# Loads of v from the third pair on issued by GpSimd instead of SyncE, in a fused attention and mixture-of-experts kernel

## The chip, the cores and the metric

The kernel runs on one core of one Trainium2 chip. The metric is the device time of one execution in microseconds (us), the median of three runs. Times inside the kernel come from one profiled execution, counted from its first instruction.

## What is computed

Four batches of 12 heads of sigmoid attention over 448 tokens, then a soft mixture of eight experts, then a dense layer with g(h) = h cos h. All inputs and outputs are float32.

```python
scores = scale * np.matmul(q, k.transpose(0, 1, 3, 2)) - np.log(S)
attn = 1.0 / (1.0 + np.exp(-scores))
x = np.matmul(attn, v)                      # (4, 12, 448, 64) -> (1792, 768)
logits = x @ phi                            # 32 slots, softmax over tokens (d) and over slots (c)
slot_out = relu((d.T @ x) @ w1) @ w2        # per expert, 4 slots each
h = (c @ slot_out) @ w_in
out = (h * np.cos(h)) @ w_out
```

## The kernel before

**Work and stages.** Two heads make a pair, and the attention stage goes through 24 pairs (`attention`, line 691). For pair i, `scores` (L395) multiplies keys and queries in four groups of keys g = 0 to 3, ScalarE applies the sigmoid (`squash`, L403), and `attn_v` (L414) multiplies with v into a single PSUM tile `av`, which VectorE copies out (`keep_tokens`, L424, the tile xt) and transposes (L431). In between, at the end of each batch of six pairs, the statistics of the slot softmax are made (L445 to L676). After the attention stage come the experts (L957 to L1088: w1, then w2, at lines 972 and 1008) and the dense layer (L1161 on).

**What is loaded, and by whom.** SyncE (SP) issues every load, and one queue takes them in that order. For each pair there are two halves of keys and queries (`load_qk`, L353, tiles raw8_1 and so on, 224 KB each, three buffers and an early one) and one tile of v (`load_v`, L357, 224 KB). VectorE splits each raw half into two float16 parts (`cast_upper` L373, tile hi, and `cast_lower` L376, tile lo). Beside that, halves of w_in (tiles wi, 512 KB, L245) and of w1 (tiles w, 512 KB, L221) are fetched ahead; each piece of wi is narrowed from float64 by one ScalarE and three VectorE operations (L264 to L271).

**The tiles of v.** Pair i's v lies in the one buffer of the pool `v_even` or `v_odd` (L313, L317, L356), so that the load for pair i + 2 has to wait until pair i's last group of `attn_v` (g = 3, with the tile `one`) has read it. From then until `attn_v` of pair i + 2 begins is the time that a load has. ScalarE also copies two corners of a loaded v (`swap_tails`, L362), which group 3 uses.

**What sets the order.** A planner (`Plan`, L73) runs through the operations with costs and ranks and emits each engine's order before the chip sees any of it. In it the load of v for pair i + 2 follows `attn_v` of group 3:

```python
824:             if i + 2 < NP:
825:                 v[i + 2] = add("sp", .62, lambda i=i: load_v(i + 2), [chain], kind="v", kb=229)
```

On the chip SP waits at each issue until the buffer is free, and what stands behind it in SP's order waits too. A later load also waits until the load eight places earlier in the same issuer's order has landed.

Of the kernel before, what the change touches and what calls it, by code (L numbers as in the profile page):

```python
# [32 lines left out]
VW = 7 * D  # L33
# [125 lines left out]
def fused(ctx: ExitStack, tc: tile.TileContext, qk, vv, phi, w1, w2, w_in, w_out, out):  # L159
    nc = tc.nc  # L160
# [148 lines left out]
    with ExitStack() as at:  # L309
# [20 lines left out]
        raw, v32, hi, lo, aa = {}, {}, {}, {}, {}  # L330
# [23 lines left out]

        def load_v(i):
            v32[i] = vps[i % 2].tile([P, VW + D], F32, tag="v", name=f"v{i}")  # L356
            nc.sync.dma_start(out=v32[i][:, 0:VW], in_=vv[i])  # L357

        def swap_tails(i, k, copy=nc.scalar.copy):

# [330 lines left out]
        def attention():  # L691
# [86 lines left out]
            for _ in range(3):  # L778
                j, m = queue.pop(0)
                qk[j, m] = add("sp", .62, lambda j=j, m=m: load_qk(j, m), [room.pop(0), qk.get("last")], kind="qk", kb=229)  # L780
                qk["last"] = qk[j, m]
            v[1] = add("sp", .62, lambda: load_v(1), kind="v", kb=229)
            fill(0)
            def score(i, g):
# [26 lines left out]
            def value(i, g):  # L811
                nonlocal chain
                swaps = None
                b, hp = divmod(i, HP)
                if g == 3:
                    for k in range(2):
                        swaps = add("act", .17, lambda k=k: swap_tails(i, k), [v.get(i), swaps if k else None], kind="swap")
                chain = av[i, g] = add(
                    "pe", (.835, .74, .74, .37)[g], lambda i=i, g=g: attn_v(i, g),
                    [chain, sq[i, g], v.get(i) if g < 3 else swaps] + ([kept.get(i - 1)] if g == 0 else []),  # L820
                )
                if g < 3:
                    return
                if i + 2 < NP:
                    v[i + 2] = add("sp", .62, lambda i=i: load_v(i + 2), [chain], kind="v", kb=229)
                kept[i] = add(
                    "dve", .54, lambda i=i: keep_tokens(i),
                    [chain, turned.get(i - 3), read.get(i - 3), ready if i == NP - 1 else None], kind="tokens",
                )
                if i < NP - 1:  # L830
                    turned[i] = add(
                        "dve", .56, lambda i=i: turn_tokens(i),
                        [kept[i], turned.get(i - 1)] + [slot.get((k, b - 1)) for k in range(2) if hp == 0],
                        kind="turn",
                    )
                if hp == 2:
                    read_tokens(b, 0)
                if hp == HP - 1 and b < B - 1 or i == NP - 2:
                    batch(b)
# [36 lines left out]
        with tc.manual_schedule():  # L876
            nc.vector.memset(zeros, 0.0)
            warm_up(8, zeros)
            for k in (1, 0):
                load_qk(0, k)  # L880
            load_v(0)
            for k in (1, 0):
                load_qk(1, k)
            nc.sync.dma_start(out=phi_sb, in_=phi)
            nc.gpsimd.memset(bias_s, neg_log_s)
            warm = const.tile([P, 1], F32, name="warm")
            nc.scalar.activation(warm, bias_s, AF.Sigmoid)
            make_identity(nc, ident)
            two = midp.tile([P, S], F32, tag="ex", name="two")[:, 0:2 * NS]
            nc.vector.tensor_add(two, ident[:, 0:2 * NS], ident[:, 2 * NS:P])  # L890
            both = [two[:, k * NS:(k + 1) * NS].unsqueeze(1).to_broadcast([P, 4, NS]) for k in range(2)]
            nc.vector.tensor_add(fold4, *both)
            first_casts()
            attention()
# [552 lines left out]
```

## Time and profile before

| | us |
|---|---|
| median of 3 runs (lowest, highest) | 506.79 (506.06, 507.98) |
| the profiled execution | 508.52 |
| its span, first to last instruction | 506.7 |
| attention stage | about 5 to 153 |
| end of attention's statistics, first weights of the experts | 153 to 164 |
| experts | 164 to 240 |
| dense layer | 240 to 507 |

The profiled execution took 1.8 us more than its span, for what lies around the first and last instruction. A row of the page or of the trace names an engine, a line of the kernel, an operation and tiles as out<-in. An idle time in brackets stands before the instruction that ended it, with what released it. PE is TensorE, PEld its weight loads, DVE VectorE, ACT ScalarE, POOL GpSimd, SP SyncE; "SPq" is SP's issue of a DMA. The three engines PE, DVE and ACT were busy for 481.8, 325.5 and 292.3 us of the span, POOL for 0.7 us.

### The profile page before, as it was taken

What the parts mean: (1) busy time and instruction counts of PE and PEld (TensorE: products, weight loads), DVE (VectorE), ACT (ScalarE), POOL (GpSimd) and SP (SyncE); (2) the same over time, 40 slices, a digit from 0 to 9 for tenths busy, and PEclk for the clock granted to TensorE, in tenths of its full rate; (3) what the DMA queues carried; (4) which work ended last, traced back from release to release, by engine and by line L of the source; (5) the groups of instructions that cost most, each with busy time, mean ns of one, the idle gap of its engine ahead of it and who ended that gap; (6) DMA issues with size and microseconds to landing.
All of it is one profiled execution on the core that took longest, in us unless ns stands there. A gap on an engine that the chain in (4) does not pass through costs nothing.

```text
span 506.7 us, 11038 instructions
## 1 busy us (share of the span) xinstructions
PE 481.8 (95%) x4560; PEld 349.3 (69%) x4560; DVE 325.5 (64%) x655; ACT 292.3 (58%) x508; POOL 0.7 (0%) x7
## 2 busy tenths in 40 slices
PE   8998989999999998677999999999999999999997
PEld 5665556565565323222567999999999899899996
DVE  4898879999975063000689899996644654654442
ACT  5887858877861002000679889865655545555552
POOL 0000000000000000000000000000000000000000
PEclk9999999999999998999999999999999999999999
DMA  7999979979839999999824633000210110020003
GB/s 254 393 314 329 295 254 358 328 225 361 278 116 378 403 417 415 413 415 389 354 56 149 232 124 125 1 2 0 76 35 1 45 64 1 26 85 0 1 0 110
DMA packets 33442, 99.12 MB, mean 196 GB/s; under 512 B 3568, under 2 KB 17520, under 8 KB 33392
## 3 DMA queue, kind: packets, MB, share of 16 engines
q1 hardware_dynamic: 33392, 98.42, 53.3%
q8 instruction: 36, 0.59, 0.5%
q14 instruction: 14, 0.11, 0.1%
HBM read 92.11 MB, written 5.51 MB: 193 GB/s over the span
## 4 chain that ended last, share of the span: by engine, by line
PE 66%; DMA 18%; DVE 11%; ACT 2%; issue 2%; SPq 0%; DVEq 0%; ACTq 0%
PE o L1234 45%; DMA w<-in_w 14%; PE av L414 6%; PE sc L395 4%; DMA raw<-in_qk 3%; PE h L1199 3%; DVE lo L376 2%; PE sl L633 2%; DVE wi L268 1%; DVE hi L373 1%; PE idle L474 1%; DVE xt L424 1%; DMA wi<-in_w_in 1%; PE o L1219 1%; PE m L945 1%
## 5 line engine op out<-in xcount | busy, mean ns | idle before, releaser
L1234 PE MATMUL o<-gh,wh 128*128 128x448 f32 x360 | 132.3, 367 | 0.4 <-DVE wi L1260 0.4
L1234 PE MATMUL o<-gl,wh 128*128 128x448 f32 x360 | 131.5, 365 | 0.0
L1234 PE MATMUL o<-gh,wl 128*128 128x448 f32 x360 | 131.5, 365 | 0.0
L403 ACT ACTIVATE a<-sc,bias_s 128x896 f32<-128x896 f32 x72 | 71.1, 1006 | 27.1 <-PE sc L395 19.6
L1234 PEld LDWEIGHTS o<-gh,wh 128*128 128x128 f32 x360 | 67.6, 188 | 7.3 <-issue 1.3
L1234 PEld LDWEIGHTS o<-gh,wl 128*128 128x128 f32 x360 | 67.6, 188 | 5.4 <-issue 0.2
L1234 PEld LDWEIGHTS o<-gl,wh 128*128 128x128 f32 x360 | 67.6, 188 | 5.3
L1212 DVE TENSOR_TENSOR gl<-wi,gh 128x448 fp32r<-128x448 f32 x60 | 37.4, 623 | 41.1 <-ACT gh L1208 37.9
L1208 ACT CAST gh<-wi 128x448 fp32r<-128x448 f32 x60 | 34.1, 568 | 51.2 <-PE o L1234 49.3
L414 PE MATMUL av<-a,v 128*64 128x224 f32 x576 | 60.4, 357 | 2.6 <-DVE xt L424 1.5
L414 PEld LDWEIGHTS av<-a,v 128*64 128x64 f32 x576 | 39.0, 137 | 23.2 <-issue 4.1
L1193 DVE TENSOR_TENSOR wi<-h,wi 128x448 f32<-128x448 f32 x63 | 39.2, 622 | 21.5 <-ACT wi L1189 21.1
L1189 ACT ACTIVATE wi<-wi 128x448 f32<-128x448 f32 x63 | 36.4, 578 | 24.8 <-DVE wi L1184 24.7
L1184 DVE SCALAR_TENSOR_TENSOR wi<-wi 128x448 f32<-128x448 f32 x63 | 39.2, 622 | 15.3 <-ACT wi L1180 15.3
L1008 PE MATMUL so<-w,zone 128*32 128x256 f32 (+1 forms) x256 | 34.2, 517 | 9.8 <-DMA w<-in_w 9.8
L395 PEld LDWEIGHTS <-hi 64*64 64x64 f16 x768 | 25.0, 107 | 21.9 <-issue 13.5
L1180 ACT ACTIVATE wi<-wi 128x448 f32<-128x448 f32 x63 | 36.5, 580 | 1.7
L395 PE MATMUL sc<-hi 64*64 64x448 f16 (+1 forms) x384 | 34.0, 342 | 2.3 <-ACT a L403 1.6
L1177 ACT ACTIVATE wi<-h 128x448 f32<-128x448 f32 x63 | 33.9, 538 | 3.8 <-PE h L1199 3.6
L395 PE MATMUL sc<-hi,lo 64*64 64x448 f16 (+1 forms) x384 | 33.3, 330 | 0.0
L395 PE MATMUL sc<-lo,hi 64*64 64x448 f16 (+1 forms) x384 | 33.1, 329 | 0.1
L1008 PEld LDWEIGHTS so<-w,zone 128*32 128x32 f32 x256 | 9.7, 114 | 31.4 <-DMA w<-in_w 20.3
(160 smaller groups left out, 552.3 us busy)
## 6 DMA issues: line engine op xcount, KB each, us to landing
w<-in_w SPq DMA_DIRECT2D x28, 768.0 KB, 15.1
w<-in_w SPq DMA_DIRECT2D x30, 512.0 KB, 5.7
wi<-in_w_in SPq DMA_DIRECT2D x24, 512.0 KB, 7.3
wo<-in_w_out SPq DMA_DIRECT2D x16, 768.0 KB, 7.0
w<-in_w SPq DMA_DIRECT2D x11, 1024.0 KB, 9.5
raw<-in_qk SPq DMA_DIRECT2D x48, 224.0 KB, 5.1
v<-in_vv SPq DMA_DIRECT2D x24, 224.0 KB, 4.9
out_t<-wi SPq DMA_DIRECT2D x24, 224.0 KB, 2.0
```

The source lines that it names most:

```text
L395: nc.tensor.matmul(ps[to, j, 0:cols.stop - cols.start], keys[at, first:first + D], q[at, cols], **flags)
L403: nc.scalar.activation(a, ps, AF.Sigmoid, bias=bias_s, scale=qk_scale)
L414: nc.tensor.matmul(av[i][rows[j], k, 0:S // 2], v32[i][at, vc:vc + D], a[at, j, sides[k] if g < 3 else slice(0, S // 2)], start=g == 0, st ...
L1008: nc.tensor.matmul(e2[g, k][j * NS:(j + 1) * NS, 0:n], h1[g][:, c, j * NS:(j + 1) * NS], w(j), start=c == 0, stop=c == F // P - 1,)
L1177: nc.scalar.activation(tmp[u][0][:, cols], hs[u][:, cols], AF.Copy, bias=0.25, scale=inv2pi)
L1180: nc.scalar.activation(tmp[u][1][:, cols], tmp[u][0][:, cols], AF.Copy, bias=magic)
L1184: nc.vector.scalar_tensor_tensor(out=ph[:, cols], in0=tn[:, cols], scalar=-magic, in1=ph[:, cols], op0=ALU.add, op1=ALU.subtract)
L1189: nc.scalar.activation(tmp[u][1][:, cols], tmp[u][0][:, cols], AF.Sin, scale=-2.0 * math.pi)
L1193: nc.vector.tensor_mul(g[:, cols], hs[u][:, cols], tn[:, cols])
L1208: nc.scalar.copy(gs[u][1], gs[u][0])
L1212: nc.vector.tensor_sub(gs[u][2], gs[u][0], gs[u][1].bitcast(F32))
L1234: nc.tensor.matmul(ps, w[:, cols], g, start=begins(u) and n == 0, stop=ends(u) and n == len(terms) - 1)
```

## The change

The loads of v for pairs 2 to 23, 22 of the 24, are issued by GpSimd. The planner still books them on SP, so that the order of everything else stays as it was.

```diff
         def load_v(i):
             v32[i] = vps[i % 2].tile([P, VW + D], F32, tag="v", name=f"v{i}")
-            nc.sync.dma_start(out=v32[i][:, 0:VW], in_=vv[i])
+            (nc.sync if i < 2 else nc.gpsimd).dma_start(out=v32[i][:, 0:VW], in_=vv[i])
```

On GpSimd the loads of v follow the making of the identity matrix, and nothing else stands between or behind them until the end. The change, on GpSimd, where the tile v2 is that of pair 2:

```order
masks.py:199 AFFINE_SELECT ident_58<-ident_58 128x128
L357 DMA v2_311<-in_vv 128x448
L357 DMA v3_410<-in_vv 128x448
L357 DMA v4_526<-in_vv 128x448
L357 DMA v5_625<-in_vv 128x448
L357 DMA v6_742<-in_vv 128x448
```

Before, GpSimd had no row after the AFFINE_SELECT until the program's last branch; 22 loads came in. On SP, before, the loads of pairs 6 to 8 stood between the halves for pairs 8 and 9 (raw8_1 is the second half for pair 8, wi_0_3_1 a tile of w_in):

```order
L353 DMA raw8_1_723<-in_qk 128x448
L357 DMA v6_742<-in_vv 128x448
L245 DMA wi_0_3_1_758<-in_w_in 128x1024
L353 DMA raw8_0_776<-in_qk 128x448
L245 DMA wi_0_3_1_758<-in_w_in 128x1024
L357 DMA v7_822<-in_vv 128x448
L245 DMA wi_0_4_0_838<-in_w_in 128x1024
```

Of these the two rows of v are gone from SP, and the others stand as they did. A little over half way through the stage, on SP, the difference at the loads for pairs 16 and 17 (w1_0_3_0 is a tile of w1):

```order
 L353 DMA raw18_1_1896<-in_qk 128x448
-L357 DMA v16_1913<-in_vv 128x448
 L221 DMA w1_0_3_0_1931<-in_w1 128x1024
 L353 DMA raw18_0_2045<-in_qk 128x448
 L353 DMA raw19_1_2053<-in_qk 128x448
 L221 DMA w1_0_3_0_1931<-in_w1 128x1024
-L357 DMA v17_2107<-in_vv 128x448
 L221 DMA w1_0_3_1_2127<-in_w1 128x1024 x2
 L353 DMA raw19_0_2159<-in_qk 128x448
```

The two halves of w1_0_3_1, and raw19_0 behind them, no longer stand behind the load of v17.

## Rows read from the trace of the kernel before

**Rows 1.** Busy time by stretch: us, each engine's busy us (x), PEclk, DMA share, GB/s

```profile
core 0: us, PE busy (x) PEld busy (x) DVE busy (x) ACT busy (x) POOL busy (x), PEclk, DMA share, GB/s
15.00:153.00 138.00, 132.41 (x2381) 81.48 (x2373) 122.44 (x310) 106.90 (x170) 0.00 (x0) 1.00 0.86 294
153.00:164.00 11.00, 10.13 (x161) 7.23 (x164) 6.69 (x20) 0.97 (x4) 0.00 (x0) 0.99 0.97 385
164.00:240.00 76.00, 64.64 (x502) 20.80 (x502) 14.33 (x26) 5.31 (x9) 0.00 (x0) 0.96 1.02 409
```

**Rows 2.** The chain that ended last, by engine (page, part 4)

```profile
PE 66%; DMA 18%; DVE 11%; ACT 2%; issue 2%; SPq 0%; DVEq 0%; ACTq 0%
```

**Rows 3.** Pieces of that chain in order of time: start us, us, what

```profile
34.93 8.39 DMA raw<-in_qk
...
48.92 0.55 DVE xt L424
...
49.51 1.00 PE av L414 x8
...
108.49 6.24 DMA raw<-in_qk
...
167.41 7.08 DMA w<-in_w
```

**Rows 4.** Who waited for whom, SP's queue: us in total, times, longest us

```profile
SPq L357 <- PE av L414: 15.8, 15, 3.1
```

**Rows 5.** The same view, the engines, from 15 to 153 us

```profile
PE av L414 <- DVE xt L424: 1.5, 4, 0.9
...
PE av L414 <- DMA v<-in_vv: 0.9, 1, 0.9
...
PE w L599 <- DVE ex L607: 0.4, 1, 0.4
```

**Rows 6.** Timeline of PE where it waited longest for v and for xt

```profile
43.95 0.41 PE L414 MATMUL av<-a,v 128*64 128x224 f32 x2 [0.94 <-DMA v<-in_vv]
...
124.52 0.41 PE L414 MATMUL av<-a,v 128*64 128x224 f32 x2 [0.88 <-DVE xt L424]
```

**Rows 7.** The instructions of line 357: SP's issues in ns, the time to landing

```profile
L357 SPq DMA_DIRECT2D v<-in_vv x24: 327/330/1125, 1.6 to 142.7; - x24
...
DMA to landing us min/median/max: 2.6/4.9/8.3
```

**Rows 8.** Timeline of PE: buffers of v freed, next used; shortest of 22, then longest

```profile
69.04 0.55 PE L414 MATMUL av<-one,v 64*64 64x224 f32 x8
...
76.12 0.41 PE L414 MATMUL av<-a,v 128*64 128x224 f32 x2
...
57.74 0.55 PE L414 MATMUL av<-one,v 64*64 64x224 f32 x8
...
71.08 0.41 PE L414 MATMUL av<-a,v 128*64 128x224 f32 x2
```

**Rows 9.** Timeline of SP around the load of v for pair 17

```profile
102.87 1.69 SPq L221 DMA_DIRECT2D w<-in_w  x1
106.01 0.33 SPq L357 DMA_DIRECT2D v<-in_vv  x1
```

**Rows 10.** Busy time by stretch, the DMA engines there

```profile
103.00:106.00 3.00, 3.00 (x49) 1.93 (x48) 2.71 (x9) 0.62 (x3) 0.00 (x0) 1.00 0.58 133
```

**Rows 11.** Timeline of DVE where it waited for raw19_0

```profile
114.75 0.39 DVE L373 CAST hi<-raw 128x448 f16<-128x448 f32 x1 [1.03 <-DMA raw<-in_qk]
```

**Rows 12.** Timeline of DVE at the first and the last of the 22 releases of v

```profile
13.35 0.62 DVE L424 COPY xt<-av 128x448 f32<-128x448 f32 x1 [2.24 <-PE av L414]
13.91 0.43 DVE L267 TENSOR_SCALAR wi<-wi 128x512 uint32<-128x512 uint32 x1
...
142.79 0.58 DVE L424 COPY xt<-av 128x448 f32<-128x448 f32 x1
143.84 0.16 DVE L612 COPY run_z<-zs 128x1 f32<-128x1 f32 x1 [0.47 <-PE zs L611]
```

**Rows 13.** Groups of DVE's instructions, 15 to 153 us: busy us, mean ns, idle before

```profile
L373 DVE CAST hi<-raw 128x448 f16<-128x448 f32 x41 | 15.4, 380 | 3.2 <-DMA raw<-in_qk 2.4 <-PE sc L395 0.6
...
L267 DVE TENSOR_SCALAR wi<-wi 128x512 uint32<-128x512 uint32 x23 | 9.6, 418 | 1.9 <-ACT wi L264 1.9
```

## The prediction, made before the changed kernel was run

> **What bounds the kernel now.** I read the busy times by stretch first, because the change touches the attention stage alone. From 15 us, just after the first moved load, to the stage's end at 153 us, TensorE is busy for 132.4 of 138.0 us and VectorE for 122.4, and the DMA engines carry a share of 0.86 [rows 1]. So TensorE bounds the stage with 5.6 us of idle time, and VectorE is close behind. After it the DMA engines take over: their share is 0.97, then 1.02 at 409 GB/s, and TensorE stands idle for 11.4 of 76 us [rows 1]. The chain that ended last hangs on weights from 167.4 us on [rows 3], and the first of them need space that attention gives back at its end. A microsecond won or lost before 153 us therefore reaches the end nearly whole. Nothing behind 153 us is changed.
>
> Next I read what the chain hangs on within the stage. By engine it is TensorE, then DMA, then VectorE; SP's queue has 0% [rows 2]. Its two long DMA pieces behind 30 us are halves of keys and queries, raw8_1 asked for at 34.9 us and raw19_0 at 108.5 [rows 3]; neither is a load of v. Last I read the waits. SP stood for 15.8 us in 15 waits until a buffer of v was free [rows 4], with loads for other engines behind it. TensorE waited for a landing v only once, 0.9 us [rows 5], at 43.95 us [rows 6].
>
> **The change, part by part.**
>
> *SP is freed.* It loses 22 issues of 0.33 us, 7.3 us [rows 7], and the 15.8 us of waits [rows 4]. By itself that is worth nothing, since SP is not on the chain [rows 2]. What counts is whether a load behind v starts earlier, on DMA engines with room, and somebody waits for it. The clearest place is at 106 us. SP is done with an issue at 102.87 + 1.69 = 104.56 and issues v17 only at 106.01 [rows 9], when its buffer is free. In the meantime the DMA engines are at a share of 0.58 over 3 us, so 1.3 us of them lie idle [rows 10]. The two tiles of w1 behind v17 will fill that hole, and raw19_0, queued behind them, will land about 1 us sooner. VectorE waits 1.03 us for it [rows 11], and that wait goes. What is late next is TensorE's wait of 0.88 us for xt from VectorE at 124.5 us [rows 6]; that is all TensorE can gain from it. **Term: 0.9 us less.**
>
> *v gets ahead of the queue.* At 43.95 us TensorE has waited 0.94 us for v6 [rows 6], and a v that doesn't stand behind SP's backlog will be there. But that gain is void. raw8_1 lands at 34.93 + 8.39 = 43.32 us, and from it a chain of VectorE's work leads to xt at 48.92 and to TensorE's next `attn_v` at 49.51 [rows 3]. A TensorE that is 0.94 us earlier waits there for xt. And the 224 KB of v6 now go out while raw8_1 is still queued: v6 came behind raw8_1 by 43.95 - 43.32 = 0.63 us, and if it passes, raw8_1 lands that much later. **Term: 0.6 us more.** Elsewhere the same exchange meets a half that nobody waits for.
>
> *v's own delivery.* The time between the release of a buffer and the first use of the next v is 69.04 + 0.55 = 69.59 to 76.12 us, 6.5 us, for the tightest of the 22 and 12.8 us for the loosest [rows 8]; read off TensorE's timeline for all of them, the median is 7.7 us. The trace shows no DMA that GpSimd issues. Bounds are the fastest and the slowest v that SP issued, 2.6 and 8.3 us to landing; I take the median of 4.9 [rows 7], because a slower issue and a queue without backlog pull in opposite directions. At 4.9 no load is late: **nothing**. At 8.3 and 0.1 us for the wait itself, 13 of the 22 would be late, by 14.5 us in all (the sum of 8.4 us less each one's time).
>
> *GpSimd beside VectorE.* What an issue on GpSimd does to VectorE no row shows. If VectorE's operations with one tensor as input, L373 and L267 [rows 13], had to stand while GpSimd issues, the cost would depend on how long it issues. I went through VectorE's timeline at the 22 releases: 0.11 us after each release GpSimd begins, and at most of them VectorE has just begun xt, 0.6 us from PSUM, as at the first and the last [rows 12], since the same last matmul releases both. Held for 0.33 us, SP's issue, the two operations lose 0.3 us over all 22; held for 1.0 us, 3.5; for 1.5, 9.3; for 2.6 us, the shortest whole delivery [rows 7], 29.6. Of VectorE's time about 0.4 is on the chain: 11% of 506.7 us is 56 us [rows 2], of some 122 busy [rows 1], a little of it outside the stage. I take the issue's 0.33 us, the one row of an issue of this very transfer: **0.1 us more**, with 11.8 us (29.6 x 0.4) as the other end, and no gain, since nothing leaves VectorE.
>
> The Trainium skill, DMA: Bandwidth & Descriptors, section Specifications, gives about 1 us to the first byte where GpSimd writes the descriptors, against about 0.6 us for SP. Read as a hold of 1.0 us, an estimate from that page, this term would be 3.5 x 0.4 = 1.4 us and the forecast 507.9 us; no run so far shows it.
>
> **Sum**: -0.9 + 0.6 + 0.1 = -0.2 us. The profiled execution of 508.52 us would become 508.3; against the median of 506.79 us that is **506.6 us**. No change that a measurement can tell: about 0.5%, or 2.5 us, is what it tells from no change here (504.3 and 509.3 us).
>
> **The rivals.**
>
> *v comes late (slower).* GpSimd takes so long to hand over a load that `attn_v` of a pair waits for its v. It decides from 6.5 us between release and landing, the tightest time [rows 8]. At 7.5 us seven loads are late by 3.9 us in all, which gives 510.7 us; at 8.4 us it is 14.5 us and 521.3. For it: SP's slowest v took 8.3 us [rows 7]. Against it: those stood behind other loads in one queue, which a queue of its own doesn't have.
>
> *GpSimd and VectorE shut each other out (slower).* The mechanism of the fourth term, with a long hold. From about 1.3 us on it costs more than 2.5 us; at 1.5 us it is 9.3 x 0.4 = 3.7 us, 510.5 us, and at 2.6 us 518.6. For it: VectorE is busy for 122 of 138 us [rows 1] and has no reserve for a pause 22 times. Against it: xt covers the first 0.6 us of nearly every hold [rows 12].
>
> This is a rule of the Trainium skill, SBUF — State Buffer, section Who interferes with whom: an operation of VectorE that streams through two ports and an instruction of GpSimd take a shared pair of ports as an exclusive lock, whoever comes first, and writing descriptors needs it. The trace of before can't show whether it holds for these loads.
>
> *Everything late becomes early (faster).* All of TensorE's waits for xt, for v and for VectorE's ex go, 1.5 + 0.9 + 0.4 = 2.8 us [rows 5], because halves and weights start sooner throughout. That gives 504.0 us. For it: the 15.8 us that SP stood in front of other loads. Against it: at a DMA share of 0.86 most of that time only made the backlog shorter, and bytes passed forward delay other bytes.
>
> *No queue of its own.* The loads of v still come out behind whatever SP has asked for. Then only who issues changes, and the time stays at 506.8 us. Against it: the order gives GpSimd its own semaphores and waits.
>
> **How the numbers follow.** The forecast has 0.58, with a range of its own from 505.9 (the gain alone) to 508.8 us (the 0.6 and a hold of 1.0 us, without the gain). Late v has 0.08, the lock with a long hold 0.18, the faster case 0.11, no queue of its own 0.05. Faster by over 0.5% is the faster case, 0.11; slower is the sum of the two slower ones, 0.26; the rest is 0.63. The range runs from 504.3 us, which leaves out most of the faster case, to 511.0 us, which takes in the lower halves of the slower ones; some 0.19 lies outside.
>
> **What would show it.** Right: rows of line 357 on POOL, landing in about 5 us; the 15.8 us gone from SP's waits; no wait of VectorE for raw19_0 near 114 us; TensorE no longer waiting for v at 44 us, but for xt at 49; L373 and L267 at 380 and 418 ns as before. Wrong: TensorE or ScalarE waiting for v in many pairs (late v); L373 or L267 longer, or VectorE idle before them without a releaser (the lock); an attention stage shorter by 2 us or more (faster). If the stage is as long as before and the end moves all the same, the passing on to the end is wrong.

## The result, and the profile after

The changed kernel took **513.59 us** (median of 4 runs, 512.24 to 517.23) against 507.34 us for the kernel before on the same chip: a ratio of 1.0127, 95% interval 1.0096 to 1.0158. It is 6.3 us slower. Run again later beside other kernels it gave 1.0137 [1.0097, 1.0177]. The forecast was no change, 506.6 us, with 511.0 us as the upper end.

I read the stretches first, as before [rows 1]; the columns are the same.

```profile
15.00:153.00 138.00, 128.81 (x2346) 79.91 (x2340) 120.97 (x308) 103.38 (x164) 11.96 (x21) 1.00 0.83 291
153.00:164.00 11.00, 10.94 (x173) 6.72 (x170) 6.40 (x18) 4.46 (x10) 0.00 (x0) 1.00 0.85 302
```

TensorE is busy for 3.6 us less in the attention stage (128.81 for 132.41), at the same granted clock of 1.00, so it idles more. The stage's last matmuls (tile lt) begin at 156.5 us instead of 152.9, and the profiled execution of 512.24 us has a span of 510.2 us, 3.5 more than before. The loss arises in attention and reaches the end whole. This execution is the fastest of the four, so that its trace holds 3.5 of the 6.3 us; what a slower one loses besides, a second trace shows further down (e10). Next the waits there, from 15 to 153 us: who waited for what, us in total, times, longest.

```profile
ACT v L362 <- DMA v<-in_vv: 6.5, 4, 2.4
...
PE sc L395 <- ACT a L403: 3.0, 2, 1.6
PE lg L452 <- ACT a L403: 2.5, 1, 2.5
...
DVE hi L373 <- DMA raw<-in_qk: 0.7, 1, 0.7
```

The engine that waits for v is ScalarE, at line 362, where it copies the two corners (`swap_tails`). In the kernel before, it waited there too, half as long:

```profile
ACT v L362 <- DMA v<-in_vv: 3.2, 3, 1.2
```

TensorE waits for sigmoids, 2.5 us at line 452 and 1.6 at line 395 (the other 1.4 us there stand at 14.8 us, at the edge of the stretch, where it waited 0.7 before). VectorE's waits for halves of keys and queries shrank from 2.4 us [rows 13] to 0.7. The timelines of ScalarE and of TensorE at the longest gap show how the first leads to the second:

```profile
78.68 0.63 ACT L403 ACTIVATE one<-sc,bias_s 128x448 f32<-128x448 f32 x1
81.75 0.50 ACT L362 COPY v<-v 64x64 f32<-64x64 f32 x2 [2.44 <-DMA v<-in_vv]
82.27 1.91 ACT L403 ACTIVATE a<-sc,bias_s 128x896 f32<-128x896 f32 x2
```

```profile
80.59 0.27 PE L395 MATMUL sc<-lo,hi 64*64 64x224 f16 x4
83.33 0.86 PE L452 MATMUL lg<-xt,phi_sb 128*32 128x128 f32 x24 [2.47 <-ACT a L403]
```

ScalarE's order has the corner copies of pair 12 ahead of the next sigmoid. The copies wait 2.44 us for v12, the sigmoid comes that much later, and TensorE, which needs it to free a bank of PSUM, waits 2.47 us. The same happens at pair 17, where the copies wait 2.29 us and TensorE 1.56. In the kernel before the same copies ran like this, on the timelines of TensorE (the release of pair 12's buffer, and of pair 17's) and of ScalarE:

```profile
74.09 0.55 PE L414 MATMUL av<-one,v 64*64 64x224 f32 x8
...
105.35 0.55 PE L414 MATMUL av<-one,v 64*64 64x224 f32 x8
```

```profile
79.02 0.50 ACT L362 COPY v<-v 64x64 f32<-64x64 f32 x2
...
110.26 0.50 ACT L362 COPY v<-v 64x64 f32<-64x64 f32 x2 [0.78 <-DMA v<-in_vv]
```

From the release (74.09 + 0.55) to the copy there were 79.02 - 74.64 = 4.38 us, and for pair 17 110.26 - 105.90 = 4.36 us, with 0.78 us of waiting in it already. These are the two tightest of the 22; pairs 22 and 15 follow with 5.5 and 5.9 us. The loads after, all instructions of line 357 (GpSimd's issues in ns; the landing of all 24):

```profile
L357 POOL DMA_DIRECT2D v<-in_vv x22: 536/536/733, 13.2 to 146.9; - x22
...
DMA to landing us min/median/max: 2.9/5.6/7.2
```

They landed a median of 5.6 us after the issue (all 24, two of them still SP's) where SP's took 4.9 [rows 7], and GpSimd's issue began 0.6 to 0.7 us after the release. That is over 6 us for places with 4.4. Gone, as was forecast, are SP's 15.8 us of waits at line 357 [rows 4] and TensorE's wait for v6 near 44 us [rows 6].

### The profile page after: what moved, and what is told of

It reads as the page before. It is cut to its first block, busy times and chain, and to the rows that moved or that the text cites. A ratio compares the mean times of both kernels' runs of the same rounds, so it can differ in the third digit from the quotient of the medians.

```text
span 510.2 us, 11065 instructions
## 1 busy us (share of the span) xinstructions
PE 482.1 (94%) x4560; PEld 349.9 (69%) x4560; DVE 325.5 (64%) x655; ACT 292.2 (57%) x508; POOL 13.4 (3%) x29
## 4 chain that ended last, share of the span: by engine, by line
PE 70%; DMA 16%; DVE 8%; ACT 4%; issue 2%; SPq 0%; ACTq 0%; DVEq 0%
PE o L1234 44%; DMA w<-in_w 12%; PE av L414 9%; PE sc L395 6%; DMA v<-in_vv 3%; PE h L1199 3%; PE h L972 2%; PE sl L633 2%; ACT a L403 2%; DVE lo L376 1%; DVE xt L424 1%; PE o L1219 1%; DMA raw<-in_qk 1%; PE m L945 1%; DVE hi L373 1%
```

## The experiments

Each ratio is against the kernel before in the same session (medians 507.5 to 508.3 us), with its 95% interval.

### Which loads carry the loss

My first theory was the corner copies: the loss sits where they stand close behind the release. The rivals were a loss spread over all loads, and the lock between GpSimd and VectorE. Two runs split the loads: pairs 9, 12, 17 and 22, where ScalarE waited for v, back on SP; and these four alone on GpSimd.

```diff
-            (nc.sync if i < 2 else nc.gpsimd).dma_start(out=v32[i][:, 0:VW], in_=vv[i])
+            (nc.sync if i < 2 or i in (9, 12, 17, 22) else nc.gpsimd).dma_start(out=v32[i][:, 0:VW], in_=vv[i])  # e1
+            (nc.gpsimd if i in (9, 12, 17, 22) else nc.sync).dma_start(out=v32[i][:, 0:VW], in_=vv[i])  # e2
```

> The loads of v for pairs 9, 12, 17 and 22 are issued by SyncE again, the other 18 by GpSimd. Corner theory: the loss comes from the four pairs for which ScalarE's copy of v's corners stands early in its order, waits for the late v and holds up the sigmoid behind it (6.5 us of waits in the changed kernel's trace, TensorE's waits of 2.5 and 1.6 us behind pairs 12 and 17). Then most of the 6.3 us come back: within 2 us of the time before, 507 to 509. Even-spread theory: each of the 22 loads costs alike, by later landings and by DMA engines shared; then 18/22 of 6.3 us stay, +5 us, about 512. Lock theory (GpSimd's issue holds up VectorE): also 18/22, and L373 or L267 over 380 and 418 ns.

> Only the loads of v for pairs 9, 12, 17 and 22 are issued by GpSimd. Corner theory: most of the loss stays, +4 to +6 us over before, with ScalarE waiting for v by about 2 us each behind pairs 12 and 17. Even-spread theory: 4/22 of 6.3 us, +1.1 us. Lock theory: +1.1 us as well.

Measured: with the four back on SP 1.0035 [1.0006, 1.0064], with the four alone on GpSimd 1.0077 [1.0056, 1.0098]. Four of 22 loads carry 0.77 of 1.27%, some six tenths of the loss, a little less than the 4 to 6 us expected. A loss spread evenly, which would be 0.23%, falls.

Two more runs moved the copies, since group 3 needs them only later: they are held until the sigmoid of the same pair's group 2 has been put out, once with the change (e3) and once with all loads on SP (e4).

```diff
+        def swap_late(i, k):
+            if i < 2 or i in squashed:
+                swap_tails(i, k)
+            else:
+                held_swaps.setdefault(i, []).append(k)
...
+            if g == 2:
+                squashed.add(i)
+                for k in held_swaps.pop(i, []):
+                    swap_tails(i, k)
```

> All 22 loads on GpSimd, as in the change; ScalarE copies the corners of a v only after the sigmoid of the same pair's group 2, which moves the copies of pairs 10, 12, 15, 16, 17, 20 and 22 a place or two back and nothing else. Corner theory: the waits of ScalarE for v in pairs 12, 17 and 22 go, and with them TensorE's of 2.5 and 1.6 us: 506 to 509 us. Even-spread and lock theories: the loads cost what they cost, 512 to 514 us. The pair with this kernel is e4_sp_late; by the corner theory the two differ by under 1.5 us, by the others by 5 or more.

> The kernel before, all loads on SyncE, with the same later copies of corners as in e3_gp_late. Before, ScalarE waited for v 3.2 us in three places (pairs 6, 10 and 17), two of which move; TensorE waited for none of these. Corner theory: 0 to 1.5 us faster than before, 505.5 to 507. The other theories say nothing of it: 507.

Measured: 1.0060 [1.0040, 1.0079] on GpSimd, 1.0009 [0.9990, 1.0028] on SP. The later copies cost nothing by themselves that the time can tell, and take half of the loss away: 510.2 us, between what the corner theory (506 to 509) and the others (512 to 514) had. The waits of e3, from 15 to 153 us, show where more is lost:

```profile
ACT v L362 <- DMA v<-in_vv: 2.1, 3, 1.2
...
PE av L426 <- DMA v<-in_vv: 1.7, 2, 1.5
...
PE sc L403 <- ACT l L478: 1.5, 1, 1.5
```

Pair 9's copies, which this edit didn't move, hold ScalarE up for 1.2 us, and TensorE stands for 1.5 us behind its next copy (line 478). TensorE itself now waits for a late v (pair 2), but it does so in e4 as well, where SP asks for every v:

```profile
PE av L426 <- DMA v<-in_vv: 1.1, 1, 1.1
```

So most of that wait comes with the later copies, and not with GpSimd. I put 2 and 9 back on SP (e7), then also 5, 12, 17 and 18 (e9), with the later copies in both:

```diff
-            (nc.sync if i < 2 else nc.gpsimd).dma_start(out=v32[i][:, 0:VW], in_=vv[i])
+            (nc.sync if i in (0, 1, 2, 9) else nc.gpsimd).dma_start(out=v32[i][:, 0:VW], in_=vv[i])  # e7
+            (nc.sync if i in (0, 1, 2, 5, 9, 12, 17, 18) else nc.gpsimd).dma_start(out=v32[i][:, 0:VW], in_=vv[i])  # e9
```

> The change with the later corner copies, and pairs 2 and 9 asked for by SP again (20 of 22 loads on GpSimd). Theory (what is left of the loss with later copies, 0.5 per cent against its twin on SP, is TensorE's wait for pair 2's v, 1.50 us, and the sigmoid behind pair 9's corner copy, 1.22 us): 508.2 us, within 0.25 per cent of the kernel before, as the twin with every load on SP (ratio 1.0009). Rival (each load through GpSimd costs something, wherever it stands, 0.1 us each): 0.45 per cent slower, 510.3 us.

> The change with the later corner copies, and pairs 2, 5, 9, 12, 17 and 18 asked for by SP again: with 20 of the loads on GpSimd, those were the pairs whose v still landed 0.7 us or less before TensorE began with it, or later than that. 16 loads stay on GpSimd. Theory (a load through GpSimd costs only where somebody waits for it): within 0.25 per cent of the kernel before, as the twin with every load on SP (ratio 1.0009). Rival (each load costs some 0.1 us wherever it stands): 0.1 x 16 = 1.6 us on top of the twin, ratio 1.004.

Measured: 1.0032 [1.0010, 1.0055] and 1.0019 [0.9997, 1.0042]. The loss falls as pairs are taken back, within intervals that overlap, and neither run parts "only the late loads cost" from "each costs some 0.1 us": both fit the intervals. A small cost of every load stays open. Part of the loss lies outside the program's span: the profiled execution of e9 took 508.55 us with a span of 506.3, 2.2 us around it where the kernel before had 1.8. Over all runs the medians of that time are 2.0 to 2.2 us in the kernels with 16 to 22 loads on GpSimd, and 1.8 to 1.9 in those with 11 or fewer.

The sharpest pair had GpSimd ask for v12, v17 and v22 alone, with the copies where they were (e12) and later (e11):

> The kernel before with the loads of pairs 12, 17 and 22 alone asked for by GpSimd, copies where they were. Theory (ScalarE's corner copies of these pairs wait for v and hold up a sigmoid and TensorE): the two gaps of TensorE behind pairs 12 and 17, 2.5 and 1.5 us, are there as with four loads, and the time is 0.6 to 0.8 per cent longer. Rival (the loss is spread over all 22 loads): 3 of 22 of 6.25 us, 0.9 us, 0.17 per cent.

> The same three loads on GpSimd, with the later corner copies. Theory: both gaps go, ScalarE no longer waits for v of these pairs, and the time is within 0.2 per cent of the kernel before. Rival (the landing is late for TensorE's matmuls as well, so that moving the copies only moves the wait): the gaps of 2.5 and 1.5 us stand before matmuls that read v, and the time is 0.6 to 0.8 per cent longer as without the later copies.

Measured: 1.0073 [1.0047, 1.0100], and with the later copies 1.0029 [1.0008, 1.0049], a little above what I had expected. TensorE's gaps of 2.65 and 1.70 us are gone in the trace of the second, and ScalarE waits for v nowhere. **For these loads the place of most of the loss is shown**: corner copies that wait for v. The 0.29% that is left isn't parted by the intervals from the 0.09% of e4.

> The change as it is, on the chip of these runs, for a closer ratio: 1.0 to 1.6 per cent slower, the interval of its first measurement.

This run of the unchanged change gave the 1.0137 told above. Its trace, of an execution of 518.05 us with a span of 516.0, shows that a wait can cost more than its length. TensorE's timeline behind pair 12's wait, the stretch from 84 to 90 us (columns as in [rows 1]), and the same matmuls in the first trace of the change:

```profile
84.33 1.51 PE L452 MATMUL lg<-xt,phi_sb 128*32 128x128 f32 x24 [3.65 <-ACT a L403]
87.04 4.23 PE L414 MATMUL av<-a,v 128*64 128x224 f32 x24
```

```profile
84.00:90.00 6.00, 5.67 (x52) 3.31 (x54) 3.81 (x18) 3.26 (x5) 0.00 (x0) 0.50 0.79 308
```

```profile
84.92 2.49 PE L414 MATMUL av<-a,v 128*64 128x224 f32 x24
```

After a wait of 3.65 us TensorE runs at a granted clock of 0.50, the lower of its two levels (1.2 instead of 2.4 GHz), and the same 24 matmuls take 4.23 us for 2.49. From the end of the wait to the end of these matmuls it is 6.94 us here and 4.08 us in the first trace; behind pair 17's wait, 2.65 us here, it is 4.86 and 3.18 us. That makes 4.5 of the 5.8 us by which this span is longer than the first. The clock also falls to 0.50 behind pair 12's wait in the traces of e2 and e12, and stays at 1.00 in those of e13 and e15. And it falls to 0.50 near 67 us in e15 and in e16, behind a wait among the matmuls of the statistics, before any moved load (in e16 there is none). So one late copy costs more in one execution than in another; how much of the medians is the clock's, one trace of each kernel doesn't show.

### Why the loads come late

Two theories were left for the landing of 5 to 7 us: weights that SP has under way at the same time, or GpSimd's own path. The first attempt took the w1 tiles out of the attention stage's list and asked for them behind it, with v on GpSimd and with v on SP:

```diff
-                while len(half) < min(2 * len(pieces) + 4, 4 + 9 * t // 8):
+                while len(half) < min(4 * KD, 4 + 9 * t // 8):
...
-            for k in range(A_SLOTS + 3 + LATE):
+            for k in range(A_SLOTS + 3 + LATE + W_SLOTS - LATE):
```

> The change, with the fourteen tiles of w1 that SP asks for during attention moved behind attention (the wi tiles stay), so that from pair 10 on, some 70 us, no weights are in SP's queue. To be compared with its twin that differs only in who asks for v. Theory A (v on GpSimd is late because its packets share the DMA engines with SP's backlog): without the backlog the loads of v for pairs 12 to 22 land in about 3 us, as pair 11's did in the change (2.9 us, first packet 1.3 us after the issue), ScalarE's waits for v in pairs 12, 17 and 22 (2.44, 2.29, 0.90 us) go, and the program is within 1 us of its twin. Rival B (asking through GpSimd takes 5 to 6 us by itself): landings stay at 5 to 6 us, the waits of about 2.3 us in pairs 12 and 17 stay, and the program is 2 to 5 us slower than its twin. Both: some 30 us slower than the kernel before, since the weights come later.

> The kernel before with the same fourteen tiles of w1 moved behind attention: the twin. Some 30 us slower than the kernel before (14 tiles of 1 MB at some 0.4 MB a microsecond, estimated 36 us less what the DMA engines had idle). Both theories: SP's loads of v for pairs 12 to 22 land in about 2.6 us (the fastest of SP's in the kernel before), and nobody waits for them.

The edit didn't do what I had written: whole tiles of w1 (1 MB) came into SP's order between the loads of attention from 57.7 us on. Until 97 us the DMA engines were full, but from 97 to 150 us only four tiles were asked for, where the changed kernel asks for 17 halves. That stretch still tells the two apart. The DMA queues and issues (KB each, median us to landing) from 97 to 150 us, in the changed kernel and in this one:

```profile
q1 hardware_dynamic: 4517, 12.49, 69.3%
q0 software_dynamic: 564, 2.01, 11.2%
...
v<-in_vv POOLq DMA_DIRECT2D x8, 224.0 KB, 5.3
```

```profile
q1 hardware_dynamic: 3392, 7.87, 45.6%
q0 software_dynamic: 576, 2.06, 13.0%
...
v<-in_vv POOLq DMA_DIRECT2D x9, 224.0 KB, 3.1
```

With SP's queue (q1) at 45.6% instead of 69.3%, GpSimd's v lands in 3.1 us instead of 5.3. So a delay of 5 us is not that of GpSimd's path by itself. The times, 1.0364 and 1.0360, are equal, but the full first half spoils both, so they decide nothing.

That left the question why so much of SP's traffic is in the way just then. SP's timeline around v12, before and after, gave the idea:

```profile
74.75 0.33 SPq L357 DMA_DIRECT2D v<-in_vv  x1
75.13 1.16 SPq L221 DMA_DIRECT2D w<-in_w  x2
```

```profile
74.34 0.90 SPq L221 DMA_DIRECT2D w<-in_w  x2
```

Before, SP stood at v12 until the buffer was free, and two halves of w1 tiles, 1 MB, followed it. After, SP doesn't stand: the same two halves go out at 74.34 us, and GpSimd asks for v12 at 75.66. **The load that was taken out of the queue is overtaken by what stood behind it.** Three runs tell this from a slow GpSimd. The first has no GpSimd in it: SP asks for the two halves ahead of v12 and v17 (e13). The second has v12 and v17 on GpSimd and holds the halves until after the next half of keys and queries (e14); the third is its twin without that (e15).

```diff
         def load_v(i):
             v32[i] = vps[i % 2].tile([P, VW + D], F32, tag="v", name=f"v{i}")
-            nc.sync.dma_start(out=v32[i][:, 0:VW], in_=vv[i])
+            load = lambda: nc.sync.dma_start(out=v32[i][:, 0:VW], in_=vv[i])  # e13
+            if i in (12, 17):
+                behind.extend([2, load])
+            else:
+                load()
...
+            (nc.gpsimd if i in (12, 17) else nc.sync).dma_start(out=v32[i][:, 0:VW], in_=vv[i])  # e14
+            if i in (12, 17):
+                held_w.append(0)
...
+        def load_half_later():
+            if held_w:
+                held_w[0] += 1
+            else:
+                load_half()
```

The comments name the runs. In e13 the load in `behind` is issued once two halves have been; in e14 `load_qk` issues the halves counted in `held_w` behind its own load.

> The kernel before, all loads on SP, but in SP's order the two halves of w1 tiles (512 KB each) that stand behind the loads of v12 and v17 now stand ahead of them. GpSimd has no part in it. Theory A (v is late because SP, which no longer stands waiting at v, asks for those weights first): v12 and v17 land 5.5 us or more after the issue instead of 3.35 and 4.22, ScalarE waits 1 to 2 us for each at the corner copy, TensorE has gaps of 1 to 2 us behind sigmoids near 80 and 114 us, and the time is 0.3 to 0.6 per cent longer. Rival B (v is late because GpSimd takes longer to ask and to hand over): landings as before within 1 us, no gaps, ratio 1.000 within 0.2 per cent.

> v12 and v17 alone on GpSimd, copies where they were, and the two halves of w1 tiles that stood behind each in SP's order held until after the next half of keys and queries. Theory A: first packet some 1.3 us after the issue, landing in about 3 us, no wait of ScalarE over 0.5 us for these two, both gaps gone, ratio within 0.2 per cent of the kernel before. Rival B: landings of 5 us or more, gaps of 2.5 and 1.5 us as with three loads, ratio 1.006 to 1.008.

> v12 and v17 alone on GpSimd, copies and weights where they were: the twin of the run with the weights held. Both theories: gaps of TensorE of 2.5 and 1.6 us near 80 and 114 us as with three loads, ratio 1.005 to 1.008 (three loads gave 1.0073).

| | who asks for v12, v17 | weights | landing, us | ratio |
|---|---|---|---|---|
| before | SP | behind v | 3.35, 4.22 | 1 |
| e13 | SP | ahead of v | 5.2, 5.7 | 1.0077 [1.0049, 1.0104] |
| e14 | GpSimd | held back | 2.9, 3.3 | 0.9978 [0.9959, 0.9998] |
| e15 | GpSimd | as in the change | 5.4, 5.2 | 1.0092 [1.0065, 1.0120] |

In e13 SP, busy with the halves, also asks for v12 only 1.0 us after the release. e13 and e15 lost a little more than expected (0.3 to 0.6 and 0.5 to 0.8%). The waits of e13, from 15 to 153 us, are those of the change, without one load on GpSimd:

```profile
ACT v L376 <- DMA v<-in_vv: 4.7, 3, 2.3
...
PE lg L466 <- ACT a L417: 1.9, 1, 1.9
...
PE sc L409 <- ACT a L417: 1.5, 1, 1.5
```

And in e14, with GpSimd, the copies of pair 12 begin without a wait, and TensorE goes on 0.05 us after its last scores (timelines of ScalarE and of TensorE):

```profile
78.39 0.50 ACT L374 COPY v<-v 64x64 f32<-64x64 f32 x2
```

```profile
79.66 0.27 PE L407 MATMUL sc<-lo,hi 64*64 64x224 f16 x4
79.98 0.86 PE L464 MATMUL lg<-xt,phi_sb 128*32 128x128 f32 x24
```

**So the cause is shown from both sides**: at pairs 12 and 17 weights ahead of v give the loss with either issuer, and with the weights held there is none, though GpSimd asks. My first words for it, that the landing is late because GpSimd delivers late, don't hold. This is the larger part of the loss; what causes the 0.35% that is left in e1, with pairs 9, 12, 17 and 22 back on SP, no run shows whole.

### The gain that was forecast, and a repair of the whole

GpSimd for v17 alone, with its copies later, is the place at which the prediction saw 0.9 us:

```diff
+            (nc.gpsimd if i == 17 else nc.sync).dma_start(out=v32[i][:, 0:VW], in_=vv[i])
```

> The kernel before with the one load v17 asked for by GpSimd, and pair 17's corner copies after the sigmoid of its group 2. It is the place at which the prediction saw its gain: SP is free to issue the two w1 tiles and raw19_0 behind v17. The prediction's first term: raw19_0 is asked for about 1 us earlier, VectorE's wait of 1.03 us at 114 us goes, and the program is 0.9 us faster, ratio 0.998. Rival (the gain is void, because TensorE next waits for v17 itself or for xt, or the bytes passed forward delay others): ratio 1.000 to 1.002, and another gap of TensorE in the same place.

Measured: 0.9993 [0.9975, 1.0011]. The time can't tell 0.9 us (0.18%) from none. In the trace raw19_0 lands 6.3 us after the release of v17's buffer where it was 8.8 before, and VectorE no longer waits for it. But a gain of TensorE doesn't follow. Its wait for xt, 0.88 us before [rows 6], is shorter by about half, and it is so in e4 as well, with the same later copies and every load on SP (timelines of TensorE in e8 and in e4):

```profile
123.61 2.49 PE L426 MATMUL av<-a,v 128*64 128x224 f32 x24 [0.47 <-DVE xt L436]
```

```profile
124.73 2.49 PE L426 MATMUL av<-a,v 128*64 128x224 f32 x24 [0.48 <-DVE xt L436]
```

In both, VectorE waits 0.59 us for a piece of w_in from ScalarE just before it comes to raw19_0.

e14 gained 0.22%. Its twin with all loads on SP and the same weights held (e16) tells whether GpSimd has a part in that; e17 and e18 hold the weights for all loads of pairs 2 to 21 on GpSimd (22 and 23 as in the change), and for pairs 11 to 21 alone.

```diff
+            nc.sync.dma_start(out=v32[i][:, 0:VW], in_=vv[i])  # e16, held: 12, 17
+            (nc.sync if i < 2 else nc.gpsimd).dma_start(out=v32[i][:, 0:VW], in_=vv[i])  # e17, held: 2 to 21
+            (nc.gpsimd if 10 < i < 22 else nc.sync).dma_start(out=v32[i][:, 0:VW], in_=vv[i])  # e18, held: 11 to 21
```

> The last version but with all loads of v on SP: the twin that holds the weights behind v12 and v17 back by one half of keys and queries, without GpSimd. If the 0.2 per cent gained with two loads on GpSimd come from SP being free earlier (the prediction's first term): ratio 1.000, slower than that version by 0.2 per cent. If they come from the order of the weights alone: ratio 0.998 as well.

> The change (all 22 loads on GpSimd), with the weights that stood behind each load of v in SP's order held until after the next half of keys and queries (pairs 2 to 21). Theory (weights passed ahead of v are the loss): landing of v down from 5.6 us median to 4 us or less, TensorE's gaps at pairs 12 and 17 gone, ratio 0.998 to 1.002 instead of 1.0137. Rival (in the first half, to 70 us, the DMA engines carry 0.95 and v is late whatever stands ahead): landings of 5 to 6 us remain there, TensorE waits for v of pair 2 or 5 and for pair 9's corners, 1.003 to 1.007.

> GpSimd asks for v of pairs 11 to 21 alone, with the weights behind each held in the same way; pairs up to 10, with the w_in tiles, and the last two stay on SP as before. Theory: landings of about 3 us, no gap of TensorE behind a corner copy, ratio 0.996 to 1.000, as with pairs 12 and 17 alone or a little better. Rival (each load through GpSimd, or each held tile, costs something): 1.001 to 1.004.

Measured: 1.0000 [0.9978, 1.0022], 1.0037 [1.0017, 1.0056] and 1.0015 [0.9993, 1.0037]. The order of the weights alone gains nothing in e16, but that doesn't make GpSimd's freeing of SP the source of e14's 0.22%: the two intervals overlap, and raw19_0 lands 4.9 us after the release in e14 and 5.1 in e16, so SP's standing at v17 doesn't make that half later. Where e14's gain comes from, if it is one, stays open. Holding the weights takes the loss of the whole change from 1.37 to 0.37%. TensorE's gap at pair 12 is gone in the trace of e17, and 0.4 us is left at pair 17. But the ratio is in the rival's range: my 4 us for the landing was wrong, the median stayed at 5.7 us, and TensorE still waits 0.9 us for v6, until 43.1 us. e18 came out in its rival's range too, with an interval that takes in both. With all weights held in turn, those of one pair may be in the way of the next; that was not tried by itself. e14 is the one version whose whole interval lies below the kernel before, at 506.77 us against 508.19, by less than the 0.5% that a measurement of this kernel tells from no change with certainty.

## Why the prediction was wrong, step by step

**What bounds the kernel: right.** TensorE bounds attention, and what it loses there reached the end: 3.6 us of TensorE's time, 3.5 us of span. Not foreseen was that a wait can cost more than its length, as in e10, where the clock fell behind it.

***v's own delivery*: wrong; this is the step that failed.** It had two halves. The deadline was taken from `attn_v`, 6.5 us at the tightest [rows 8], and the first use of v is ScalarE's corner copy, after 4.4 us at the tightest. The copy was named in the description of the kernel and in the planner's order; that TensorE doesn't read its result until group 3 hid that ScalarE's sigmoids stand behind it. ScalarE's 3.2 us of waits for v in the kernel before were the row to read; the prediction read TensorE's alone. And the time to landing was taken as 4.9 us [rows 7], with the words that a queue of its own has no backlog: it was 5.6, with 0.6 to 0.7 us before the issue, for which 0.11 had been taken. With the right deadline even SP's median would have warned: 4.9 us is 0.5 us more than the two tightest copies have, and with the 0.6 us before the issue they are late by 1.1 us each. The term that was put at nothing came to 4.0 us of TensorE's waits in the first trace (2.47 + 1.56).

***v gets ahead of the queue*: wrong in its sign.** It forecast that v6 would pass raw8_1 and make it 0.6 us later. In the change raw8_1 lands at 40.4 us, 5.3 us after its issue instead of 8.4, and v6 behind it, at 42.2. TensorE's wait near 44 us did go, and 0.78 us for VectorE's lo at 48.9 took its place, but that doesn't prove the term: in e13, e14 and e16, where SP asks for v6, TensorE doesn't wait for v6 either, and waits 0.7 us for lo. Why both loads were so slow in the trace of the kernel before, no run shows. Where it mattered, at v12 and v17, v was passed instead. The step *SP is freed* holds the sentence that should have warned me: the two tiles of w1 behind v17 "will fill that hole". They did, and v17, asked for after them, came behind them. I counted what the freed queue gains and not whom it overtakes.

***SP is freed*: the half comes sooner, the gain is not shown.** In the change VectorE's wait for raw19_0 [rows 11] is gone, and a longer one for a piece of w_in from ScalarE, which the corner copies had held up, stands just before it:

```profile
117.47 0.43 DVE L267 TENSOR_SCALAR wi<-wi 128x512 uint32<-128x512 uint32 x1 [1.50 <-ACT wi L264]
117.81 0.39 DVE L373 CAST hi<-raw 128x448 f16<-128x448 f32 x1
```

With v17 alone (e8) raw19_0 landed 2.5 us sooner, counted from the release, but TensorE's next wait was no shorter than in e4. Of the time that SP won, most went into waiting for a buffer of keys and queries instead (SP's queue, before and after, us in total, times, longest):

```profile
SPq L353 <- DVE lo L376: 29.2, 25, 2.7
```

```profile
SPq L353 <- DVE lo L376: 45.8, 24, 5.3
```

The Trainium skill, DMA: Bandwidth & Descriptors, section Issuing engines are not separate DMA queues, says that starting transfers from several engines only saves the time on the issuing sequencer, since all of them end up on the same 16 DMA engines. The traces agree that SP's time is what the change won. It was more than the issues themselves, 15.8 us of waits [rows 4] beside 7.3 us of issues [rows 7], and before v12 SP used it to put 1 MB ahead.

***GpSimd beside VectorE*: right, near nothing.** The groups of [rows 13] after, from 15 to 153 us:

```profile
L373 DVE CAST hi<-raw 128x448 f16<-128x448 f32 x41 | 15.4, 380 | 1.4 <-DMA raw<-in_qk 0.7 <-PE sc L395 0.6
...
L267 DVE TENSOR_SCALAR wi<-wi 128x512 uint32<-128x512 uint32 x23 | 9.6, 417 | 5.2 <-ACT wi L264 5.2
```

380 and 417 ns, where it was 380 and 418; the longer idle time of L267 is ScalarE's. If anyone is held it is GpSimd: an issue with a cast that begins 0.2 us into it takes 0.72 us instead of 0.54 (timelines of GpSimd and of VectorE):

```profile
70.61 0.54 POOL L357 DMA_DIRECT2D v<-in_vv  x1 [11.06 <-PE sc L395]
75.66 0.72 POOL L357 DMA_DIRECT2D v<-in_vv  x1 [4.51 <-PE sc L395]
```

```profile
75.86 0.39 DVE L373 CAST hi<-raw 128x448 f16<-128x448 f32 x1 [0.21 <-PE sc L395]
```

Not every overlap does this: the issue at 41.34 us has a cast from 41.37 on and takes 0.54 us.

**The rivals.** *v comes late* is what happened, at a chance of 0.08; its place (`attn_v`), its point of decision (6.5 us) and its price were all taken from the wrong reader of v. The lock, the faster case and *No queue of its own* fell, the last by GpSimd's rows in a queue q0; but what it said of the loads, that they still come out behind whatever SP has asked for, was nearer to the truth than my forecast.

## What to carry to other kernels

Before a load changes its queue, list every engine that reads the tile, with the time from the buffer's release to the first read on each, and what stands behind that read in the engine's order: a small copy on a side engine can be the deadline. A load that stands waiting in an in-order queue also holds back everything behind it, and so keeps the DMA engines clear for itself; take it out, and the transfers behind it go first. If it is moved all the same, the large transfers that stood behind it have to be kept behind it. And price a wait of TensorE by what follows it too: where the clock fell behind one, the next matmuls took 1.7 times as long.

## What the runs showed of the hardware

A load that GpSimd had asked for moved nothing for 3.3 us while SP's queue was full. GpSimd asks for v12 at 75.66 us in the change; from 75.7 to 78.9 us the DMA engines moved packets of SP's queue alone, at a share of 0.91:

```profile
DMA packets 289, 0.91 MB, mean 284 GB/s; under 512 B 30, under 2 KB 96, under 8 KB 289
...
q1 hardware_dynamic: 289, 0.91, 91.2%
```

Its own came from 79.0 us on, and it landed at 81.72. With the weights held (e14) it asks at 74.70 us. The DMA engines' busy tenths from 74.7 to 77.7 us, in slices of 0.075 us:

```profile
DMA  9997521000000000000969693529353110057728
```

They run dry after 0.5 us and start again in the twentieth slice, some 1.4 us after the issue, and v lands at 77.64. What holds GpSimd's packets for two further microseconds when the engines are full, no run here shows.

The Trainium skill, DMA: Bandwidth & Descriptors, section Specifications, gives about 1 us to the first byte on GpSimd's path. The idle case agrees in size, with 1.4 us from the start of an issue of 0.75; under load it was 3.3 us.
